# A state-space convolution beside grouped attention: the output projection of the last queries is summed ahead of the last norm

## The chip, the cores and the metric

The program runs on one core of a Trainium2 chip. Its time is device microseconds from launch to end. TensorE (PE in the profile) multiplies, VectorE (DVE) and ScalarE (ACT) work on elements, GpSimd (POOL) has a few small steps, and SyncE (SP) issues DMA transfers. Products land in PSUM, eight banks of 128 x 512 fp32.

## The reference, cut to what matters

Two independent halves are computed from two inputs of 2048 x 640 and written side by side.

```python
# A: diagonal state-space layer, complex
Lam_bar = exp(dt * Lam);  B_bar = ((Lam_bar - 1) / Lam)[:, None] * Bmat
h[t] = Lam_bar * h[t-1] + (x @ B_bar.T)[t]          # 2048 steps
a = 2 * real(h @ Cmat.T) + x * Dskip
# B: 32 query heads of 20, one key and one value head
q = (x @ wq) as 32 heads;  k = x @ wk;  v = x @ wv
p = softmax(q @ k.T * 20 ** -0.5)                   # 32 x 2048 x 2048
b = concat_heads(p @ v) @ wo
out = concat([a, b], -1)                            # 1 x 2048 x 1280, bf16
```

## The kernel before, in words

**Attention.** Queries are cut into four blocks of 512 (`qb`), heads into eight groups of four (`gg`). One block of 512 queries and four heads is a block `b` (32 of them), and has 64 score tiles of 128 keys x 512 queries, 2048 tiles in all; `tile_n` counts them. TensorE multiplies keys and queries into the score banks: slot SC0 has three banks, slot SC1 two. ACT takes a whole slot in one exponential (line 1000) and writes bf16 weights to one of seven buffers PR. About one tile in five goes to a miscellaneous bank instead, where DVE makes the exponential by integer arithmetic (line 553: one instruction from PSUM, three corrections from SBUF, into buffers DR). TensorE multiplies all weights by the values, four heads side by side, into the bank `pvbank` (MB2), with one column for the softmax's denominator.

**Norm.** When a block's 64 tiles are summed, DVE copies the bank to `pvsb` (line 1190). For 31 blocks the denominators travel through DRAM and back (`normalize`, four DMA steps) and DVE multiplies them in, `norm_op[b]`, into a buffer OT. For the last block it is done on the chip, to be quicker: `den_task` brings the denominators to rows (product with E1), DVE takes the reciprocal, POOL spreads each of the 16 numbers of a row over 32 columns (rdT to rdX, line 1244), `norm_task` turns that back with a product with ident, and DVE multiplies.

**Output projection.** `o_task(qb, k, bank)` makes one output tile: k = 0 to 3 are 128 rows x 512 columns, k = 4 is the last 128 columns of all four row blocks. Each sums over the eight groups `gg` with products of OT and WO4. A product with 128 stationary columns is issued as four of 32 columns side by side (`mm`, line 528). `finish` copies the bank to one of four staging buffers (DVE, line 1298) and issues the write on SP (line 1301).

**State-space half.** Per block of 512 time steps: `unit_task` (inputs by B, rotated, scanned on DVE) and `y_task` (states by C, `finish`).

**What sets the order.** Nothing is looped at run time: `Schedule.run` plays the program with fixed durations, and each engine picks the ready step of lowest `prio` (ties by age). What it picked becomes the static instruction list of each engine, and `Emitter` adds the semaphore waits. An engine then runs its list strictly in order. Scores have priority 0, exponentials 0.5, attention products 2.0 (`PV`, line 1056), background products 1.6 (`TASK`). `background` lists the background tasks with the tile number from which they may start; state-space tasks are spread from tile `SSM_FROM` to `SSM_TO`. `manager` gives a task one of two miscellaneous banks; while one is in use the second goes only to tasks overdue by `OVERDUE` tiles. `keep_source` (line 603) adds filler products (VZ by KT, 256 columns) where TensorE's load of the last 3 us is under `KEEP`.

In this order, before, the end is: last exponential, three attention products, the copy to pvsb, the norm's steps, then all five output tiles of the last block, their copies and writes in turn in the two miscellaneous banks.

Of the kernel before, what the change touches and what calls it, by code (L numbers as in the profile page):

```python
# [8 lines left out]
ACT = mybir.ActivationFunctionType  # L9
# [350 lines left out]
NQB, NKC, NGG = 4, 16, 8  # L360
NTILE = NQB * NGG * NKC * 4
# [5 lines left out]
class Build:  # L367
# [230 lines left out]
                  load=512.0, deps=[self.zero_op], reads=["PR0"], writes=[self.pvbank.key], hook=self.warm_last)  # L598


    KEEP = 3200.0

    def keep_source(self):

# [3 lines left out]
        if self.pv_filled[b] == 64 and sum(len(q) for q in self.pvq[b]) < 12:  # L608
            return None
        if self.s.recent(3000.0) > self.KEEP:  # L610
            return None
# [334 lines left out]
    def attention(self):  # L946
# [10 lines left out]
        while self.tile_n < NTILE:  # L957
# [14 lines left out]
            fill = self.pe([], self.mmt(512, 2), deps=deps, prio=0, mode="S", hook=lambda op, i=i: self.fill(op, i))  # L972
            k += 1

    def fill(self, op, i):
        p = self
        t, banks = self.slots[i]
        n = min(self.CHUNKS[i], NTILE - self.tile_n)
        h = self.hold[self.nhold % self.NPS]
        self.nhold += 1  # L980
        tiles = list(range(self.tile_n, self.tile_n + n))
        self.tile_n += n
        extra = []
        while len(tiles) < 4 - len(extra) and self.want_d(len(extra)):
            tiles.append(self.tile_n)
            self.tile_n += 1
            extra.append(min(tiles, key=self.d_weight))
            tiles.remove(extra[-1])
            self.d_per[extra[-1] // 64, extra[-1] % 4] += 1
        ents = []  # L990
        for x, m in enumerate(tiles):
            b, kc, j = self.score(op, m, t[:, 512 * x:512 * x + 512], banks[x])
            ents.append((b, kc, j, p.PR[:, h.index, x, :]))
        for m in extra:
            self.fill_d(op, m)
        op.reads = sorted(set(op.reads))
        op.dur = self.mmt(512, len(op.fns))
        op.load = 128.0 * len(op.fns)
        dst = p.PR[:, h.index, 0:n, :]
        ex = self.act(lambda e: e.activation(dst, t[:, 0:512 * n], ACT.Exp, scale=1.0 / UNIT),  # L1000
                      0.8333 * 512 * n + 50,
                      deps=[op], reads=[b.key for b in banks[:n]], writes=[f"PR{h.index}"], prio=0.5,
                      gate=lambda: not h.taken or (h.left == 0 and self.s.done(h.users)))

        def on_start(_):
            h.taken, h.left, h.users, h.waits = True, n, [], False
        h.waits = True
        ex.hook = on_start
        self.slot_last[i] = [ex]
        for b, kc, j, rhs in ents:  # L1010
            self.pvq[b][j].append((p.VP[:, kc, 0:32], kc, rhs, f"PR{h.index}", ex, h, "VP"))
            self.pv_filled[b] += 1
# [217 lines left out]
    def den_task(self, b, bank):  # L1230

        p = self
        slot = b % 2
        src = p.pvsb[:, slot, :]
        m1 = self.pe([self.mm(bank.cols(4 * i, 4 * i + 4), src[:, 128 * i:128 * i + 128], p.E1[:], True, True)
                      for i in range(4)], 4 * 65, deps=[self.evac_op[b], self.c_op["E1"]] + bank.last, prio=1.5,
                     reads=[f"pvsb{slot}", "E1"], writes=[bank.key])

        def rc(e):
            with p.nc.allow_low_precision("bf16 reciprocal of softmax denominator"):  # L1240
                return e.reciprocal(p.rdT[:], bank.cols(0, 16))
        r = self.dve(rc, 170, deps=[m1], reads=[bank.key], writes=[f"rdT{slot}"], prio=0.45)
        spread = bass.AP(tensor=p.rdT, offset=0, ap=[[16, 128], [1, 16], [0, 32]])
        self.spread_op[b] = self.pool(lambda e: e.tensor_copy(p.rdX[:], spread), 700, deps=[r],
                                      reads=[f"rdT{slot}"], writes=[f"rdX{slot}"], prio=1)
        yield lambda: r.start is not None
        bank.last = [r]
        self.give(bank)
# [16 lines left out]
        self.give(bank)  # L1265

    def o_task(self, qb, k, bank):
        p = self
        ops = self.o_ops.setdefault(qb, [])
        prev = None  # L1270
        ots = [(8 * qb + gg) % 10 for gg in range(NGG)]
        deps = [self.norm_op[8 * qb + gg] for gg in range(NGG)] + [self.wo_op] + bank.last
        if k < 4:
            for gg in range(NGG):
                prev = self.pe([self.mm(bank.ap, p.OT[:, ots[gg], 128 * k:128 * k + 128], p.WO4[:, gg, 0:512], gg == 0,
                                        gg == NGG - 1)], self.mmt(512), deps=deps, prev=prev, prio=self.task_prio(),
                               reads=[f"OT{ots[gg]}", "WO4"], writes=[bank.key])
            rows = self.out[0, 512 * qb + 128 * k:512 * qb + 128 * k + 128, 640:1152]
        else:
            for ts in range(4):  # L1280
                for gg in range(NGG):
                    prev = self.pe([self.mm(bank.cols(128 * ts, 128 * ts + 128),
                                            p.OT[:, ots[gg], 128 * ts:128 * ts + 128], p.WO4[:, gg, 512:640], gg == 0,
                                            gg == NGG - 1)], 65, deps=deps, prev=prev, prio=self.task_prio(),
                                   reads=[f"OT{ots[gg]}", "WO4"], writes=[bank.key])
            rows = self.out[0, 512 * qb:512 * qb + 512, 1152:1280].rearrange("(t p) n -> p t n", p=128)
        ev = self.finish(prev, rows, bank, ops)
        yield lambda: ev.start is not None
        self.give(bank)

    def finish(self, prev, rows, bank, ops):

        ops.append(prev)
        i = self.outs % 4
        self.outs += 1
        key, st = f"stg{i}", self.stg[:, i, :]
        last = self.stage_dma.get(key)
        ev = self.dve(lambda e: e.tensor_copy(st, bank.ap), 620, deps=[prev], reads=[bank.key], writes=[key], prio=self.EV,  # L1298
                      gate=(lambda: last.end is not None and last.end + 100 < self.s.t) if last else None)
        src = st if len(rows.shape) == 2 else st.rearrange("p (t n) -> p t n", t=4)  # L1300
        self.stage_dma[key] = self.dma(lambda e: e.dma_start(rows, src), 131072, f"out{i}", deps=[ev], reads=[key],
                                       prio=1)
        bank.last = [ev]
        return ev

# [237 lines left out]
        return lambda: o is None or o.start is not None  # L1543


    SSM_FROM, SSM_TO = 130, 1960

    def background(self):
        T = self.tasks
        for qb in range(NQB):  # L1550
            for gg in range(NGG):
                t = -100 + gg if qb == 0 else (qb - 1) * 512 + 40 + 50 * gg
                T.append((t, 1, lambda b=8 * qb + gg: self.tile_n >= 64 * (b - 11), lambda bank, qb=qb, gg=gg: self.qt_task(qb, gg, bank)))
                if gg % 4 == 3:
                    T.append((t + 0.5, 0, lambda qb=qb, gg=gg: self.row_ready(qb, gg),
                              lambda bank, qb=qb, gg=gg: self.row_task(qb, gg // 4, bank)))
# [3 lines left out]
                T.append((64 * (b + 1), 0, lambda b=b: self.norm_ready(b), lambda bank, b=b: self.norm_task(b, bank)))  # L1560
        for qb in range(NQB):
            for k in range(5):
                T.append((512 * (qb + 1) + 30 + 40 * k, 2, lambda qb=qb: self.o_ready(qb),
                          lambda bank, qb=qb, k=k: self.o_task(qb, (4, 0, 1, 2, 3)[k], bank)))
        jobs = []
        for tb in range(NQB + 1):
# [29 lines left out]
        return self.ot_free(b)  # L1596

    def o_ready(self, qb):
        return all((8 * qb + gg) in self.norm_op and self.norm_op[8 * qb + gg].start is not None for gg in range(NGG))

    def unit_ready(self, tb, c, ri):
        if ri == 1:
# [11 lines left out]
        return all((tb, c) in self.w_op and self.w_op[(tb, c)].start is not None for c in range(NC))  # L1614

    in_use = 0
    OVERDUE = 80

    def manager(self):
        tasks = self.tasks  # L1620

        def choose():
            if not any(b in self.misc for b in self.free_banks):
                return None
            late = self.tile_n - self.OVERDUE if self.started and self.in_use > 0 else 1e9
            best = None
            for i, (t, cls, ok, gen) in enumerate(tasks):
                if t > self.tile_n and self.tile_n < NTILE:
                    break
                if t > late and cls > 0:  # L1630
                    continue
                if (best is None or cls < tasks[best][1]) and ok():
                    best = i
            return best
        while tasks:
            yield lambda: choose() is not None
            i = choose()
            bank = self.take(self.misc)
            self.in_use += 1
            bank.task = True  # L1640
            _, _, _, gen = tasks.pop(i)
            self.s.spawn(gen(bank))
            yield lambda: True
# [50 lines left out]
```

## Time and profile before

| | us |
|---|---|
| median of 7 runs (lowest, highest) | 801.0 (800.76, 805.16) |
| the profiled execution | 801.24 |
| its span, first to last instruction | 799.5 |
| ACT busy | 769.8 |
| TensorE busy, DVE busy | 731.5, 729.8 |
| POOL busy | 14.1 |
| mean granted TensorE clock | 0.998 of full |

The span lies 1.7 us under the profiled execution's own time, and that 0.24 above the median. Busy times are sums over stages with different limits; records of one engine can overlap, since a following instruction starts while the one ahead drains. A profile line gives source line, engine, operation, written tile <- read tiles, shape, count, then busy time and mean ns of one. Line 538 holds nearly all products of the helper `mm`, line 534 those issued in fours, so they are told apart by their tiles: SC and MB are banks, WO,OT the output projection, PR,VP and DR,VS attention sums, E,pvsb and ident,rdX the last norm.

### The profile page before, as it was taken

The numbers are of one execution on the slowest core, as the hardware profiler recorded it, in microseconds if no ns is written. First come the engines' busy times: TensorE is split into PE (matmuls) and PEld (weight loads), VectorE is DVE, ScalarE is ACT, GpSimd is POOL, SyncE is SP. The second block draws the span as 40 slices with busy tenths as digits, with TensorE's granted clock in tenths as the row PEclk, the third lists the DMA queues.
The fourth block names the chain that finished last, engine by engine and source line by source line (L and its number), as shares of the span: only waits on it lengthen the run. The fifth ranks groups of instructions, "written<-read, shape, count | busy, mean of one in ns | idle before, by whom it ended". The sixth has DMA issues, their size and how long they took to land.

```text
span 799.5 us, 23698 instructions
## 1 busy us (share of the span) xinstructions
PE 731.5 (91%) x10175; PEld 237.8 (30%) x10177; DVE 729.8 (91%) x1779; ACT 769.8 (96%) x689; POOL 14.1 (2%) x36
## 2 busy tenths in 40 slices
PE   7989898989889999999899999999988999989986
PEld 3322222222224233222323223223222322223323
DVE  5999999999998988998998999999999899997692
ACT  5899999999999999999999999999999999999991
POOL 6000000000000000000000000000000000000000
PEclk9999999999999999999999999999999999999999
DMA  9830020000001000010000000020000100000101
GB/s 206 128 77 8 17 43 9 7 4 10 8 9 24 22 16 22 16 33 25 15 2 23 22 23 23 5 45 16 10 15 9 29 15 22 15 9 16 29 16 35
DMA packets 54185, 21.57 MB, mean 27 GB/s; under 512 B 43464, under 2 KB 54080, under 8 KB 54080
## 3 DMA queue, kind: packets, MB, share of 16 engines
q1 hardware_dynamic: 52072, 19.87, 11.5%
q8 instruction: 80, 1.31, 0.7%
q10 hardware_dynamic: 2008, 0.18, 0.3%
q14 instruction: 25, 0.20, 0.1%
HBM read 7.20 MB, written 5.50 MB: 16 GB/s over the span
## 4 chain that ended last, share of the span: by engine, by line
issue 96%; PE 1%; DVE 1%; DMA 1%; ACTq 0%; POOL 0%; POOLq 0%; DVEq 0%
PE MB L534 1%; DMA vrow<-in_A_Dskip_dram 1%; DVE xbT L760 0%; DVE fr L553 0%; POOL fr L553 0%; ACTq L519 0%; DVE wq L748 0%; DVE OT L548 0%; DVE stg L1298 0%; POOLq L425 0%; DVE aq L552 0%; DVE mab L781 0%; ACTq L518 0%; DVE sc L552 0%; DVE trig L552 0%
## 5 line engine op out<-in xcount | busy, mean ns | idle before, releaser
L1000 ACT ACTIVATE PR<-SC 128x1536 bf16<-128x1536 f32 (+1 forms) x667 | 754.7, 1459 | 4.7 <-PE SC L538 2.5
L538 PE MATMUL SC<-QT,KT 32*128 32x512 bf16 x1668 | 259.9, 384 | 53.0 <-ACT PR L1000 42.3
L553 DVE TENSOR_SCALAR DR<-MB 128x512 int16<-128x512 f32 x380 | 255.2, 685 | 29.3 <-PE MB L538 27.5
L538 PE MATMUL MB<-PR,VP 128*32 128x512 bf16 x1668 | 250.9, 385 | 1.7 <-DVE pvsb L1190 0.7
L538 PE MATMUL MB<-DR,VS 128*32 128x512 bf16 x1520 | 247.0, 384 | 0.7 <-DVE DR L553 0.4
L553 DVE TENSOR_SCALAR DR<-DR 128x512 int16<-128x512 int16 (+1 forms) x849 | 238.3, 333 | 4.0 <-PE MB L538 1.8
L538 PEld LDWEIGHTS SC<-QT,KT 32*128 32x128 bf16 x1668 | 66.9, 91 | 307.9 <-ACT PR L1000 243.4
L538 PE MATMUL MB<-QT,KT 32*128 32x512 bf16 x380 | 139.7, 384 | 1.9 <-DVE DR L553 1.4
L538 PEld LDWEIGHTS MB<-PR,VP 128*32 128x32 bf16 x1668 | 60.6, 94 | 65.8 <-issue 51.7
L538 PEld LDWEIGHTS MB<-DR,VS 128*32 128x32 bf16 x1520 | 59.6, 94 | 56.4 <-issue 42.6
L534 PE MATMUL MB<-xaT,BT 128*32 128x512 bf16 x800 | 61.6, 382 | 0.6 <-DVE QT L881 0.3
L548 DVE TENSOR_TENSOR prod<-MB,Z 128x1024 bf16<-128x1024 f32 x40 | 48.8, 1221 | 5.6 <-PE MB L534 5.3
L538 PE MATMUL MB<-xbT,wqf 128*32 128x512 bf16 x640 | 48.5, 382 | 0.4 <-DVE QT L881 0.3
L534 PE MATMUL MB<-WO,OT 128*32 128x512 bf16 (+1 forms) x1024 | 46.9, 311 | 0.4 <-DVE OT L548 0.4
L538 PEld LDWEIGHTS MB<-QT,KT 32*128 32x128 bf16 x380 | 33.0, 91 | 22.0 <-issue 10.7
L1470 DVE TENSOR_TENSOR_SCAN g<-sc,hst,u 128x512 bf16<-128x512 f32 x30 | 37.9, 1276 | 0.0
L1298 DVE CAST stg<-MB 128x512 bf16<-128x512 f32 x40 | 27.4, 686 | 8.1 <-PE MB L534 7.9
L538 PE MATMUL MB<-KT,VZ 128*32 128x256 bf16 x628 | 32.9, 275 | 0.0
L534 PE MATMUL MB<-CT,xbT 128*32 128x512 bf16 (+1 forms) x640 | 31.0, 300 | 0.1
L534 PE MATMUL MB<-CT,W 128*32 128x512 bf16 (+1 forms) x640 | 30.5, 301 | 0.0
L548 DVE TENSOR_TENSOR prod<-g,tab 128x1024 bf16<-128x1024 bf16 x40 | 27.1, 681 | 0.1
L1190 DVE CAST pvsb<-MB 128x512 bf16<-128x512 f32 x32 | 21.9, 686 | 4.0 <-PE MB L538 3.5
(116 smaller groups left out, 332.3 us busy)
## 6 DMA issues: line engine op xcount, KB each, us to landing
out_dram<-stg SPq DMA_DIRECT2D x40, 128.0 KB, 1.8
rdB<-recs SPq DMA_DIRECT2D x124, 32.0 KB, 1.9
CT<-in_B_x_dram SPq DMA_DIRECT2D x2, 640.0 KB, 5.6
WO<-in_B_wo_dram SPq DMA_DIRECT2D x4, 200.0 KB
wqf<-in_B_wq_dram SPq DMA_DIRECT2D x1, 680.0 KB, 5.9
sums<-pvsb SPq DMA_DIRECT2D x31, 4.0 KB
dn<-sums SPq DMA_DIRECT2D x31, 4.0 KB, 2.0
recs<-rc SPq DMA_DIRECT2D x31, 4.0 KB, 1.6
```

Of the source, the lines that this page charges most:

```text
L534: r = e.matmul(out[32 * j:32 * j + 32], lhsT=lhsT[:, 32 * j:32 * j + 32], rhs=rhs, start=start, stop=stop, tile_position=(0, 32 * j), skip ...
L538: return lambda e: e.matmul(out, lhsT=lhsT, rhs=rhs, start=start, stop=stop, **kw)
L548: return lambda e: e.tensor_tensor(out, a, b, op)
L553: return lambda e: e.tensor_scalar(out, a, s1, s2, op0=op0, op1=op1)
L1000: ex = self.act(lambda e: e.activation(dst, t[:, 0:512 * n], ACT.Exp, scale=1.0 / UNIT), 0.8333 * 512 * n + 50, deps=[op], reads=[b.key fo ...
L1190: ev = self.dve(lambda e: e.tensor_copy(p.pvsb[:, slot, :], bank.ap), 620, deps=[op], reads=[bank.key], writes=[f"pvsb{slot}"], prio=self. ...
L1298: ev = self.dve(lambda e: e.tensor_copy(st, bank.ap), 620, deps=[prev], reads=[bank.key], writes=[key], prio=self.EV, gate=(lambda: last.e ...
L1470: o = self.dve(lambda e, ri=ri, init=init: e.tensor_tensor_scan(p.g[:, u, ri, :], rdec, p.u[:, ri, :], init, ALU.mult, ALU.add), 1280, dep ...
```

## The change

- Output tiles of the last query block (`last`, qb = 3) may start once the first group is normed, from tile 2040 on, and each group's products wait for that group's norm alone. k = 4 goes group by group instead of row block by row block. The products have priority 2.5 (1.4 for the last group).
- After the last scores of a slot have been taken by ACT, the slot's banks join the miscellaneous ones, so more output tiles can be open at once. The limit by `OVERDUE` is off for the last eight tiles.
- The last block's output is staged in the free buffers PR, one for each tile. Three of the five copies (k = 4, 1, 3) are made by ACT, two by DVE.
- The spread of the reciprocals (rdT to rdX) goes from POOL to DVE.
- `KEEP` 3200 to 3500, `SSM_FROM, SSM_TO` 130, 1960 to 110, 1830, `OVERDUE` 80 to 120.

```diff
-    KEEP = 3200.0
+    KEEP = 3500.0
...
+        for i in (k % 2, (k + 1) % 2):
+            yield lambda: fill.start is not None and all(o.start is not None for o in self.slot_last[i])
+            for bank in self.slots[i][1]:
+                bank.last, bank.busy = list(self.slot_last[i]), False
+                self.misc.append(bank)
+                self.free_banks.append(bank)
...
-        self.spread_op[b] = self.pool(lambda e: e.tensor_copy(p.rdX[:], spread), 700, deps=[r],
+        self.spread_op[b] = self.dve(lambda e: e.tensor_copy(p.rdX[:], spread), 350, deps=[r],
...
+        last = qb == NQB - 1
+        def part(gg, prev):
+            fns = []
+            for ts in range(4) if k == 4 else [k]:
+                out, w = (bank.cols(128 * ts, 128 * ts + 128), p.WO4[:, gg, 512:640]) if k == 4 else (bank.ap, p.WO4[:, gg, 0:512])
+                fns.append(self.mm(out, p.OT[:, ots[gg], 128 * ts:128 * ts + 128], w, gg == 0 and ts in (0, k), gg == NGG - 1))
+            return self.pe(fns, 4 * 65 if k == 4 else self.mmt(512), deps=[self.norm_op[8 * qb + gg], self.wo_op] + bank.last,
+                           prev=prev, prio=1.4 if last and gg == NGG - 1 else 2.5 if last else self.task_prio(),
+                           reads=[f"OT{ots[gg]}", "WO4"], writes=[bank.key])
+        for gg in range(NGG):
+            if last:
+                yield lambda: 8 * qb + gg in self.norm_op
+            prev = part(gg, prev)
...
-        ev = self.finish(prev, rows, bank, ops)
+        ev = self.finish(prev, rows, bank, ops, k if last else None)
...
+        else:
+            key, st = f"PR{end}", self.PR[:, end, 0, :]
...
+        if end in (4, 1, 3):
+            ev = self.act(lambda e: e.activation(st, bank.ap, ACT.Copy), 600, deps=[prev], reads=[bank.key], writes=[key], prio=1)
...
-    SSM_FROM, SSM_TO = 130, 1960
+    SSM_FROM, SSM_TO = 110, 1830
...
-                T.append((512 * (qb + 1) + 30 + 40 * k, 2, lambda qb=qb: self.o_ready(qb),
+                T.append((512 * (qb + 1) + 30 + 40 * k if qb < NQB - 1 else NTILE - 8, 2, lambda qb=qb: self.o_ready(qb),
...
-        return all((8 * qb + gg) in self.norm_op and self.norm_op[8 * qb + gg].start is not None for gg in range(NGG))
+        ggs = range(NGG if qb < NQB - 1 else 1)
+        return all((8 * qb + gg) in self.norm_op and self.norm_op[8 * qb + gg].start is not None for gg in ggs)
...
-    OVERDUE = 80
+    OVERDUE = 120
...
-            late = self.tile_n - self.OVERDUE if self.started and self.in_use > 0 else 1e9
+            late = self.tile_n - self.OVERDUE if self.started and self.in_use > 0 and self.tile_n < NTILE - 8 else 1e9
```

More of the change, by code (lines that the diff above doesn't have):

```diff
@@ L1271, in o_task @@
         ots = [(8 * qb + gg) % 10 for gg in range(NGG)]
-        deps = [self.norm_op[8 * qb + gg] for gg in range(NGG)] + [self.wo_op] + bank.last
+        last = qb == NQB - 1
[7 more added lines that the diff above has]
+                           reads=[f"OT{ots[gg]}", "WO4"], writes=[bank.key])
@@ L1273, in o_task @@
+        for gg in range(NGG):
+            if last:
+                yield lambda: 8 * qb + gg in self.norm_op
+            prev = part(gg, prev)
         if k < 4:
[L1274 to L1277, printed above, removed]
@@ L1278, in o_task @@
             rows = self.out[0, 512 * qb + 128 * k:512 * qb + 128 * k + 128, 640:1152]
         else:
[L1280 to L1285, printed above, removed]
@@ L1286, in o_task, with finish @@
             rows = self.out[0, 512 * qb:512 * qb + 512, 1152:1280].rearrange("(t p) n -> p t n", p=128)
-        ev = self.finish(prev, rows, bank, ops)
+        ev = self.finish(prev, rows, bank, ops, k if last else None)
         yield lambda: ev.start is not None
         self.give(bank)
-    def finish(self, prev, rows, bank, ops):
+    def finish(self, prev, rows, bank, ops, end=None):
         ops.append(prev)
-        i = self.outs % 4
-        self.outs += 1
-        key, st = f"stg{i}", self.stg[:, i, :]
-        last = self.stage_dma.get(key)
-        ev = self.dve(lambda e: e.tensor_copy(st, bank.ap), 620, deps=[prev], reads=[bank.key], writes=[key], prio=self.EV,
-                      gate=(lambda: last.end is not None and last.end + 100 < self.s.t) if last else None)
+        if end is None:
+            i = self.outs % 4
+            self.outs += 1
+            key, st = f"stg{i}", self.stg[:, i, :]
+        else:
+            key, st = f"PR{end}", self.PR[:, end, 0, :]
+        last = self.stage_dma.get(key)
+        if end in (4, 1, 3):
+            ev = self.act(lambda e: e.activation(st, bank.ap, ACT.Copy), 600, deps=[prev], reads=[bank.key], writes=[key], prio=1)
+        else:
+            ev = self.dve(lambda e: e.tensor_copy(st, bank.ap), 620, deps=[prev], reads=[bank.key], writes=[key], prio=self.EV,
+                          gate=(lambda: last.end is not None and last.end + 100 < self.s.t) if last else None)
@@ L1300, in finish @@
         src = st if len(rows.shape) == 2 else st.rearrange("p (t n) -> p t n", t=4)
-        self.stage_dma[key] = self.dma(lambda e: e.dma_start(rows, src), 131072, f"out{i}", deps=[ev], reads=[key],
-                                       prio=1)
+        self.stage_dma[key] = self.dma(lambda e: e.dma_start(rows, src), 131072, f"out{key}", deps=[ev], reads=[key], prio=1)
         bank.last = [ev]
```

## The prediction

> **What bounds the kernel now.** I read the page first, then the groups kept apart by shape, then the timeline of the last 20 us engine by engine, then windows of the TensorE clock.
>
> ```profile
> PE 731.5 (91%) x10175; PEld 237.8 (30%) x10177; DVE 729.8 (91%) x1779; ACT 769.8 (96%) x689; POOL 14.1 (2%) x36
> ```
>
> ScalarE (ACT) leads, but 91% on two others says little before the stages are separated. In the groups (busy, mean ns | idle before, by whom):
>
> ```profile
> L1000 ACT ACTIVATE PR<-SC 128x1536 bf16<-128x1536 f32 x334 | 557.5, 1669 | 4.0 <-PE SC L538 2.5 <-PE MB L538 1.4
> L1000 ACT ACTIVATE PR<-SC 128x1024 bf16<-128x1024 f32 x333 | 415.4, 1247 | 0.6 <-PE MB L538 0.6
> ...
> L538 PEld LDWEIGHTS SC<-QT,KT 32*128 32x128 bf16 x1668 | 66.9, 91 | 307.9 <-ACT PR L1000 243.4 <-DVE DR L553 40.0 <-issue 10.3
> ```
>
> From 25.33 us (first exponential) to 782.55 (last) ACT runs 667 exponentials with hardly a gap, and TensorE waits for ACT before new scores: the main stage is ACT's. Overlapping records hide part of its loss. Start to start, the trace never has under 1.330 us after a three-bank exponential nor under 0.904 after a two-bank one: 333 pairs x 2.234 = 743.9 us, against 780.79 - 25.33 = 755.5. So 11.5 us of waiting lie in the main stage (the longest single one 1.24 us, near 487). After it:
>
> ```profile
> 778.54 4.01 ACT L1000 ACTIVATE PR<-SC 128x1536 bf16<-128x1536 f32 x3
> ```
> ```profile
> 782.61 0.40 PE L538 MATMUL MB<-PR,VP 128*32 128x512 bf16 x3 [0.51 <-ACT PR L1000]
> 783.80 0.26 PE L534 MATMUL MB<-E,pvsb 128*32 128x4 bf16 x16 [0.79 <-DVE pvsb L1190]
> 785.12 0.41 PE L534 MATMUL MB<-ident,rdX 128*32 128x128 bf16 x16 [1.06 <-POOL rdX L1244]
> 785.36 0.56 PE L534 MATMUL MB<-WO,OT 128*32 128x128 bf16 x28
> 786.33 10.13 PE L534 MATMUL MB<-WO,OT 128*32 128x128 bf16 x228 [0.40 <-DVE OT L548]
> ```
> ```profile
> 785.58 0.69 DVE L548 TENSOR_TENSOR OT<-pvsb,MB 128x512 bf16<-128x512 bf16 x1 [1.19 <-PE MB L534]
> 789.21 0.69 DVE L1298 CAST stg<-MB 128x512 bf16<-128x512 f32 x1 [2.94 <-PE MB L534]
> 791.33 0.69 DVE L1298 CAST stg<-MB 128x512 bf16<-128x512 f32 x1 [1.43 <-PE MB L534]
> 793.05 0.69 DVE L1298 CAST stg<-MB 128x512 bf16<-128x512 f32 x1 [1.03 <-PE MB L534]
> 794.78 0.69 DVE L1298 CAST stg<-MB 128x512 bf16<-128x512 f32 x1 [1.03 <-PE MB L534]
> 796.50 0.69 DVE L1298 CAST stg<-MB 128x512 bf16<-128x512 f32 x1 [1.03 <-PE MB L534]
> ```
>
> Call the end of the last exponential E = 782.55. The tail is 799.52 - 782.55 = 16.97 us with ACT idle: 3.78 to the first product after the last norm, 10.13 of output products, 0.05 + 0.69 for the last copy, 2.32 for the last write and the closing waits. Part of the 10.13 ran on half a clock (below).
>
> **The tail, in the changed kernel's order.** The built order is a list, and says which products stand ahead of which wait. I price it in groups of four column-tiled products. A 512-column group is 1.72/8 = 0.216 us (a round of eight groups between two copies above). A 128-column group is (785.36 - 785.12)/4 = 0.06, by start to start 0.056, and twice that on half a clock.
>
> (1) Before E. The exponential before the last ends at E - 1.34. Behind it TensorE has one attention group (0.22), 16 output groups of 128 columns (0.89) and one of 512 (0.22): with the hop of 0.05 done at about E + 0.03. The last attention products, which wait for E, are reached just in time; if they are late, that adds one to one.
>
> (2) Last attention products. Before, three stood behind E (one group); now thirteen, four groups: TensorE free at E + 0.05 + 0.86 = E + 0.91, the sum complete near E + 1.09 instead of E + 0.45. Cost 0.64. DVE's copies that they also wait for should be done by E - 1 (nine DVE instructions, 4.3 us of rows, follow a score filled at about E - 6.8).
>
> (3) Norm. Output groups now fill the three gaps of the chain, five each time, 1.08 us: behind the attention sum, behind the small product with E1, behind the product with ident. The old gaps were 0.79 + 0.22, 1.06 and 0.40 + 0.56 us, so the fillings are a little longer than the waits and TensorE sets the pace: E1 at 0.91 + 1.08 = E + 1.99, +0.11, +1.08, ident at E + 3.18, +0.23, +1.08: ready for the last norm at E + 4.49. The chain by itself, 783.00 to 786.33 = 3.33 less what the spread saves, would be ready at 1.09 + 3.12 = E + 4.21; so 4.49 holds.
>
> (4) The spread moves from POOL (0.61) to DVE. No row is a copy that repeats each element 32 times. Bounds: 0.29 (the 128x512 int16 form of line 553) and 0.69 (a 512-column cast); I take 0.42, the two-operand bf16 row of line 548, as it lies between: 0.2 saved. At 0.69 it would be about 0.2 later than the filling, otherwise hidden by it. [...] No row here shows the case, and the sum changes by at most 0.2.
>
> (5) After the last norm. The words of the change promise one group of each output tile; the order gives more. Of the third 512-wide tile only two of the seven earlier groups stand ahead of the norm's wait, of the fourth none; they are queued behind it though they do not need it. So: 4 groups of 128 (0.22), 1 + 7 + 8 = 16 groups of 512 (3.45), 0.17 for the last result: E + 8.33. Before: 796.46 = E + 13.91.
>
> (6) Copies and writes. Three copies go to ACT (0.59 by the 128x512 copy of line 763), two to DVE; each result is further from the next than a copy takes, or goes to the other engine, so only the last counts: 0.05 + 0.59, E + 8.97. SP issues five writes of 0.33 to 0.40 us in this order, none late. The staging names grow from 4 to 9, so SP's closing waits (two names per instruction, 0.06 each) grow by at most 0.15; I take 0.1. End: E + 8.97 + 2.32 + 0.1 = E + 11.4. Tail 16.97 - 11.4 = **5.6 us less**.
>
> The clock of the tail is a second term: full clock is assumed above. Windows of before show (us, TensorE busy, granted clock, DMA share, GB/s):
>
> ```profile
> 786.80:787.30 0.50, 0.50 (x31) 0.50 0.00 0
> 787.30:787.80 0.50, 0.50 (x32) 0.50 0.17 33
> ...
> 789.30:789.80 0.50, 0.50 (x9) 0.50 0.00 0
> 789.80:790.30 0.50, 0.50 (x16) 1.00 0.00 0
> ```
>
> Half speed from about 786.4 to 789.8, after 3.4 us with many gaps; it cost 3.4/2 = 1.7 us. With the gaps filled I expect none of it; if it comes all the same, 1.7 is to be added. [...]
>
> **The main stage.** The counts do not move: 334 + 333 exponentials and 380 scores on DVE in both orders, so ACT's floor of 743.9 stays. What moves is the waiting of 11.5 us:
> - Fillers rise from 628 to 892, 66 more groups of 0.12 us = 7.9 us of TensorE. They stand where it would idle (it waits 243 us for ACT). The clock was 1.00 all through, so they buy nothing; a filler in the wrong place costs one 0.12.
> - DVE: 82 more single copies (0.287) and 41 fewer double (0.420): +6.3 us; three copies fewer in the tail, -2.1; one spread, +0.4. From 729.8 to about 734 of the 757 us of the stage: covered, but the cover is thin, 98.0 of 100 us in the window from 100 to 200.
> - The state-space work (about 179 us of DVE by its rows) goes into 1720 tiles instead of 1830, at 0.37 us a tile 636 us instead of 676: 28% of DVE instead of 26.5% there, less after it. Its writes move earlier through SP, 0.35 us each, past the norm chains' small transfers.
> - TensorE's work between two score fills, counted from both orders with the prices above: 22 pairs of fills longer than ACT's 2.234 us before, 26 after, with about the same excess.
>
> None of this fixes the sign. I take zero, bounds -4 (a third of the waits goes) and +4.
>
> **Sum.** Against the profiled execution (801.24 us for a span of 799.5): 801.2 - 5.6 = 795.6; the median of the seven runs is 0.24 lower, so **795.4**.
>
> **Rivals.**
> A (0.62): as above, the main stage within 2.4 us of before: 793 to 798.
> B (0.16): the looser end of the state-space work also takes waits out of the main stage, 4 of the 11.5: 791.4. For it: the six waits of 0.5 us and more make 4.6 us, and lie where that work is dense. Against: the work is packed denser there.
> C (0.13): the gain is there and eaten: the half clock in the tail (1.7) and 2 us of new waits, 795.4 + 3.7 = 799.1, no change. For it: steps 1 to 3 leave no slack.
> D (0.09): slower. DVE becomes the bound in the stretch of the denser state-space work, at 100 to 650 us: late copies hold back attention products, these hold the exponentials' buffers, ACT waits. If the 11.5 us double, 795.4 + 11.5 = 806.9. It decides once it takes 5.6 + 2.4 = 8 us. Against: the order gives DVE no more scores than before.
>
> A measurement of this kernel can tell about 0.3%, 2.4 us. Faster by more: A and B, 0.78; within: 0.13; slower: 0.09. The range takes in the bounds of the main stage: 795.4 - 4 and 795.4 + 4 with some of C: 791.5 to 799.8.
>
> **What would show it.** In the changed profile: the tail from the last exponential about 11.4 us; the first product after the norm about E + 4.5 and 3.7 us of output products behind it; PEclk 1.00 there; rdX on DVE near 0.42; the last exponential ending within 2.4 us of 782.55. I am wrong if that end moves by more than 4 us, if the clock halves again, or if the thirteen attention products start later than E + 0.3.

## The result and the profile after

| | before | after |
|---|---|---|
| median, us (lowest, highest; runs) | 801.29 (799.65, 805.16; 45) | 798.36 (795.95, 802.12; 17) |
| ratio of the times, with its 95% interval | | 0.9958 [0.9948, 0.9968] |
| the profiled execution | 801.24 | 799.93 |
| its span | 799.52 | 798.20 |
| of it: up to the first exponential | 25.33 | 25.37 |
| main stage, first exponential to the end E of the last | 757.22 | 761.62 |
| tail, E to the last instruction | 16.97 | 11.21 |

The change makes the kernel 0.42% faster; 0.7% was forecast. The last three rows say where the rest is: the tail is 5.75 us shorter, and the main stage, which the change was not about, is 4.40 us longer.

The page's busy times, and the exponentials kept apart by shape (count | busy, mean ns | idle before, by whom):

```profile
PE 736.5 (92%) x10439; PEld 240.6 (30%) x10441; DVE 732.0 (92%) x1818; ACT 772.2 (97%) x692; POOL 13.5 (2%) x35
```
```profile
L1007 ACT ACTIVATE PR<-SC 128x1536 bf16<-128x1536 f32 x334 | 555.4, 1663 | 6.8 <-PE SC L538 4.8 <-PE MB L538 2.0
L1007 ACT ACTIVATE PR<-SC 128x1024 bf16<-128x1024 f32 x333 | 413.1, 1240 | 1.6 <-PE MB L538 1.0 <-PE SC L538 0.6
```

The same 334 + 333 exponentials, so ACT's floor of 743.9 us stands; the idle time before them grew from 4.6 to 8.4 us. By starts (over 1.330 and 0.904 us) the waits are 15.99 us against 11.54.

**The tail.** TensorE's timeline from E = 786.99 on (start, us, source <- tiles, count):

```profile
787.04 0.39 PE L538 MATMUL MB<-PR,VP 128*32 128x512 bf16 x1
...
787.72 1.45 PE L534 MATMUL MB<-WO,OT 128*32 128x512 bf16 x18
788.89 0.31 PE L534 MATMUL SC<-E,pvsb 128*32 128x4 bf16 x10
...
789.26 1.09 PE L534 MATMUL SC<-WO,OT 128*32 128x512 bf16 x16
790.14 0.44 PE L534 MATMUL SC<-ident,rdX 128*32 128x128 bf16 x16
790.37 1.28 PE L534 MATMUL SC<-WO,OT 128*32 128x512 bf16 x20
791.45 0.64 PE L534 MATMUL MB<-WO,OT 128*32 128x128 bf16 x20
791.89 3.44 PE L534 MATMUL SC<-WO,OT 128*32 128x512 bf16 x60
```

No line has an idle time in brackets, where before there were four: WO,OT fills the three gaps of the norm's chain, and 80 products (20 groups) are left behind the norm. DVE's spread and ACT's last copy:

```profile
789.65 0.43 DVE L1251 COPY rdX<-rdT 128x512 bf16<-128x512 bf16 x1
```
```profile
795.38 0.60 ACT L1314 ACTIVATE PR<-SC 128x512 bf16<-128x512 f32 x1 [2.37 <-PE SC L534]
```

**The main stage.** The long waits of ACT stand at new places: 1.03, 1.04 and 1.00 us at 63.6, 65.5 and 68.8, then 0.99 and 1.34 at 96.9 and 100.5. Windows of 3.41 us (TensorE busy, granted clock, DMA share, GB/s):

```profile
55.81:59.22 3.41, 3.41 (x50) 1.00 0.04 8
59.22:62.63 3.41, 2.21 (x31) 1.00 0.02 1
62.63:66.04 3.41, 3.41 (x27) 0.50 0.12 41
66.04:69.45 3.41, 3.41 (x30) 0.50 0.00 0
69.45:72.86 3.41, 3.33 (x45) 1.00 0.02 5
...
93.36:96.77 3.41, 2.21 (x31) 1.00 0.24 65
96.77:100.18 3.41, 3.41 (x34) 0.50 0.71 132
```

Twice TensorE is busy for only 2.21 of 3.41 us, and the clock is half for one or two windows after it: a fill of two score banks then takes 0.60 us (0.39 at full clock), and ACT waits. Before, the main stage had no window at half clock. What TensorE lacked in the two thin windows is in the timelines of SP, DVE and TensorE:

```profile
56.96 0.51 SPq L1215 DMA_DIRECT2D dn<-sums  x1
```
```profile
60.37 0.34 DVE L1220 RECIPROCAL rc<-dn 64x32 bf16<-64x32 bf16 x1 [1.36 <-DMA dn<-sums]
...
92.16 2.19 DVE L683 MEMSET WO<- 128x2560 uint32 x1 [0.48 <-issue]
```
```profile
62.18 0.38 PE L538 MATMUL MB<-QT,KT 32*128 32x512 bf16 x1 [1.01 <-DVE QT L881]
...
95.48 0.38 PE L538 MATMUL MB<-QT,KT 32*128 32x512 bf16 x1 [1.01 <-DVE DR L553]
```

First: a block's denominators took 3.4 us from issue to landing (2.4 before). DVE reaches the reciprocal 2.05 us after the issue, about as before (2.16), so it waits 1.36 us (0.27 before), is late with the copies behind it (QT and DR), and TensorE idles 1.01 us. So here the late landing made the wait, and not the reciprocal's place in the list. Second: DVE zeroes WO4 in 2.19 us, where `Schedule.run` counted 1.5. DVE's exponential that frees a miscellaneous bank stands behind that (94.74 us), and TensorE idles 1.01 us before the next score for that bank.

The 17 times go with the granted clock: the four runs at clock 1.000 took 795.95 to 796.38 us, five at 0.996 took 798.3 to 798.67, two of the three at 0.994 took 799.93 and 799.99. One window at half rate is 0.002 of the mean clock (half of 3.41 us in 798), so each goes with 1.0 to 1.3 us, its cause included. Most times around the median are those of runs with two (the median run itself, 798.36 us at 0.998, shows one).

### The profile page after: what moved, and what is told of

Read it like the earlier page. It is cut to its first block, busy times and chain, and to the rows that moved or that the text cites. A ratio compares the mean times of both kernels' runs of the same rounds, so it can differ in the third digit from the quotient of the medians.

```text
span 798.2 us, 24288 instructions
## 1 busy us (share of the span) xinstructions
PE 736.5 (92%) x10439; PEld 240.6 (30%) x10441; DVE 732.0 (92%) x1818; ACT 772.2 (97%) x692; POOL 13.5 (2%) x35
## 3 DMA queue, kind: packets, MB, share of 16 engines
q8 instruction: 82, 1.34, 0.7%
## 4 chain that ended last, share of the span: by engine, by line
ACT 82%; PE 10%; DVE 5%; DMA 1%; issue 1%; SPq 0%; ACTq 0%; DVEq 0%
ACT PR L1007 82%; PE MB L538 4%; PE SC L538 3%; DVE DR L553 3%; PE MB L534 2%; PE SC L534 1%; DMA vrow<-in_A_Dskip_dram 1%; DVE prod L548 0%; DMA dn<-sums 0%; SPq L927 0%; DVE WO L683 0%; DVE xbT L760 0%; DMA sums<-pvsb 0%; ACTq L519 0%; DVE fr L553 0%
## 5 line engine op out<-in xcount | busy, mean ns | idle before, releaser
L553 DVE TENSOR_SCALAR DR<-MB 128x512 int16<-128x512 f32 x380 | 255.3, 685 | 24.8 <-PE MB L538 22.9
L538 PE MATMUL MB<-PR,VP 128*32 128x512 bf16 x1668 | 254.4, 386 | 1.5 <-DVE pvsb L1197 1.3
L538 PE MATMUL MB<-DR,VS 128*32 128x512 bf16 x1520 | 254.2, 387 | 0.6 <-DVE pvsb L1197 0.6
L553 DVE TENSOR_SCALAR DR<-DR 128x512 int16<-128x512 int16 (+1 forms) x890 | 243.2, 325 | 7.7 <-PE MB L538 4.5
L534 PE MATMUL MB<-xaT,BT 128*32 128x512 bf16 x800 | 62.9, 387 | 0.0
L538 PE MATMUL MB<-KT,VZ 128*32 128x256 bf16 x892 | 43.5, 276 | 0.0
L534 PE MATMUL MB<-WO,OT 128*32 128x128 bf16 (+1 forms) x928 | 42.4, 292 | 0.0
L538 PEld LDWEIGHTS MB<-QT,KT 32*128 32x128 bf16 x380 | 33.1, 91 | 22.2 <-issue 12.1
L1316 DVE CAST stg<-MB 128x512 bf16<-128x512 f32 x35 | 23.9, 684 | 3.9 <-PE MB L534 3.5
L538 PEld LDWEIGHTS MB<-KT,VZ 128*32 128x32 bf16 x892 | 22.1, 96 | 12.7 <-issue 6.4
```

Source lines behind the costliest of these rows:

```text
L534: r = e.matmul(out[32 * j:32 * j + 32], lhsT=lhsT[:, 32 * j:32 * j + 32], rhs=rhs, start=start, stop=stop, tile_position=(0, 32 * j), skip ...
L538: return lambda e: e.matmul(out, lhsT=lhsT, rhs=rhs, start=start, stop=stop, **kw)
L553: return lambda e: e.tensor_scalar(out, a, s1, s2, op0=op0, op1=op1)
```

## The experiments

Theory 1: the tail's edits bring all of the forecast, and the three constants (`KEEP`, `SSM_FROM`/`SSM_TO`, `OVERDUE`) give part of it back in the main stage, by places like these two. Rivals: the tail's new order itself disturbs the main stage; or DVE becomes the bound where state-space work is packed denser (rival D).

**e1: the tail's edits alone.** The three constants as before, and the earlier query blocks' output tiles in their old order (the change's new loop also reorders their k = 4).

```diff
-    KEEP = 3500.0
+    KEEP = 3200.0
-    SSM_FROM, SSM_TO = 110, 1830
+    SSM_FROM, SSM_TO = 130, 1960
-    OVERDUE = 120
+    OVERDUE = 80
+        if not last:   # the old loops, row block by row block, all norms at once
+            ...
-        for gg in range(NGG):
+        for gg in range(NGG) if last else []:
```

> Only the tail edits (output tiles of the last queries ahead of the last norm, score banks given back, staging in PR, copies on two engines, spread on DVE); KEEP, SSM_FROM, SSM_TO and OVERDUE as before, and earlier query blocks' output tiles in their old order. The instruction lists of all engines are those of the kernel before up to TensorE's instruction 9836 of 10162. Theory 1 (the tail gives its gain, the three constants lose some of it in the main stage): last exponential ends within 1 us of 782.6; behind it one attention group instead of four in the changed kernel, so the tail is 16.97 - 10.5 = 6.4 us shorter than before; ratio 0.992, and better than the changed kernel's 0.9958. Theory 2 (the tail edits themselves hold the main stage up): last exponential near 787 and a ratio near 0.996.

Measured: 794.6 us, ratio 0.9927 [0.9915, 0.9938]. Waits 11.61 us at the places of before, main stage 757.30 (before 757.22), tail 10.56. The tail's edits cost the main stage nothing. The tail is also 0.65 us shorter than in the changed kernel: one group of attention products stands behind E here, not four.

**e2: the constants alone**, in the kernel before.

```diff
-    KEEP = 3200.0
+    KEEP = 3500.0
-    SSM_FROM, SSM_TO = 130, 1960
+    SSM_FROM, SSM_TO = 110, 1830
-    OVERDUE = 80
+    OVERDUE = 120
```

> The kernel before with only the constants of the change: KEEP 3500, SSM 110 to 1830, OVERDUE 120. Theory 1: main stage 2 to 4.5 us longer, half-rate windows of TensorE in the first 110 us in most runs, tail as before: ratio 1.003 to 1.005. Theory 2: 1.000.

Measured: 803.06 us, ratio 1.0032 [1.0020, 1.0045]. In its profile the main stage is 1.25 us longer than before (waits 1.02 and 1.14 us at 93.9 and 97.3, half clock from 94.3 to 97.7) and the tail 0.74 (a second window at half clock). 2 to 4.5 us of main stage were expected, so that part was missed. The parts add up in time: -0.73% and +0.32% make -0.41%, and the whole change measured -0.42%. They do not add up place by place, since the 0.74 us lie in a tail that the changed kernel does not have, so that the sum is this close is in part chance.

**e3: the second place mended.** The changed kernel, same order; DVE zeroes five of the eight parts of WO4, GpSimd the other three.

```diff
-        ... self.dve(lambda e: e.memset(p.WO4[:], 0.0), 1500, writes=["WO4"], ...
+        ... self.dve(lambda e: e.memset(p.WO4[:, 0:5, :], 0.0), 1500, writes=["WO4"], ...
+        self.pool(lambda e: e.memset(p.WO4[:, 5:8, :], 0.0), 2000, writes=["WO4b"], ...
```

> The changed kernel, all instruction lists of TensorE, DVE and ACT unchanged, but the zeroing of WO4 on DVE (2.19 us near 92 us, which the planner counts as 1.5) is cut to five eighths of its columns, about 1.4 us; GpSimd zeroes the rest early. Theory 1 with this instruction as one of its causes: TensorE's idle time of 1.0 us near 94.5 shrinks to 0.3 or less, the clock stays 1.00 from 96 to 101, and ACT's two waits there (0.99 and 1.34) go: 1 to 2.3 us faster than the changed kernel, ratio 0.993 to 0.995. Rival: the clock halves there for another reason, or the time is lost elsewhere later: ratio 0.996 unchanged.

Measured: 796.51 us, ratio 0.9947 [0.9936, 0.9959]. The profile has no window at half clock, waits 11.16 us, main stage 756.79, tail 11.21. TensorE has no idle time of 1 us near 94, so the second place is mended. The waits near 63 to 71 are gone too, though nothing was done for them: with the same lists the transfer to dn took 1.9 us here and not 3.4, and the reciprocal waited for nothing. So the first place depends on when that transfer lands. All five runs show a clock of 0.998 or 1.000, as 7 of the 17 of the changed kernel do; but the two ratios' intervals overlap, so the gain in time is likely and not shown beyond the noise. The edit also costs something: the first exponential starts at 26.43 us, 1.06 late. While GpSimd zeroes its part of WO4 (from 18.34 us, for 1.69), one of DVE's instructions ahead of the first scores (line 553, into fr) takes 2.48 us, where the same one took 0.85 in the changed kernel; in e5, with the same edit, it takes 2.49.

**e4: the first place mended in the plan.** `Schedule.run` counts the transfer to dn 1 us longer, so that the reciprocal is planned later.

```diff
-                     reads=[f"sums{b}"], writes=[dn], prio=1)
+                     reads=[f"sums{b}"], writes=[dn], prio=1, land=1000.0)
```

> The changed kernel, but the planner counts the second transfer of the denominators (sums to dn) as landing 1 us later, so that DVE's reciprocal stands later in its list and the list is no longer held up when the transfer is late (1.36 us near 59 in the profiled run). The order of everything behind changes. Theory 1 with this wait as one of its causes: no wait of DVE for dn, no half-rate window near 62 to 69, ACT's three waits there (1.03, 1.04, 1.00) go: ratio 0.992 to 0.994. Rival (each new order brings its own waits): those waits go and others come, ratio 0.996 plus or minus 0.003.

Measured: 801.23 us, ratio 1.0005 [0.9993, 1.0016]: worse than either reading. The order is another one throughout. DVE takes 372 scores and not 380, so ACT does 8 more (about 8 x 0.45 = 3.6 us), and there are waits of 0.73, 0.63 and 0.64 us at 62.9 to 67.4 around a window at half clock all the same. Nor did the edit do what it was for: the transfer took 1.8 us, but was issued later (58.69 us), DVE reached the reciprocal 0.51 us after the issue and waited 1.33 us for it. So e4 says nothing on what the first place is worth.

**e5: e1 with e3's edit.**

```diff
-        ... self.dve(lambda e: e.memset(p.WO4[:], 0.0), 1500, writes=["WO4"], ...
+        ... self.dve(lambda e: e.memset(p.WO4[:, 0:5, :], 0.0), 1500, writes=["WO4"], ...
+        self.pool(lambda e: e.memset(p.WO4[:, 5:8, :], 0.0), 2000, writes=["WO4b"], ...
```

> The tail edits alone (as e1_tail_pure), and the zeroing of WO4 on DVE cut to five eighths, the rest early on GpSimd; no list of TensorE or ACT changes. If DVE's late zeroing also causes the waits of the exponentials near 100.0 (0.75) and 104.4 (0.77) that e1 and the kernel before share, both go: 1 to 1.5 us less than e1, ratio 0.991. If it causes only the first: 0.992. If neither: 0.9927 as e1.

Measured: 796.7 us, ratio 0.9939 [0.9923, 0.9956]. Of the two waits of 0.75 us at 100 and 104 one is gone, but the waits in sum (11.68 us against 11.61) and the main stage (757.37 against 757.30) are those of e1, and the first exponential comes 1.46 us later (26.38 against 24.92), by e3's side effect. So this edit brings e1 nothing and costs the late start.

**e6: e1 without fillers.**

```diff
-    KEEP = 3200.0
+    KEEP = -1.0
```

> The tail edits alone, without any filler products (612 in e1, none here); the planner's order changes from TensorE's instruction 468 on. The prediction's view (the fillers buy nothing where the clock is full): clock 0.998 or more, time within 0.3% of e1, ratio 0.990 to 0.996. Rival (the fillers hold the clock up): half-rate windows in the main stage, at 1.2 to 1.4 us each; with four or more of them a clock of 0.99 and a ratio of 0.998 or more.

Measured: 815.38 us, ratio 1.0163 [1.0136, 1.0189]. 612 filler products less, and mean clock, waits (34.5 us) and main stage (779.30 us) are all worse:

```profile
core 0: 815.2 us, clock 0.952
```

A clock of 0.952 over 815.2 us is worth 23 windows of 3.41 us at half clock. The waits grew by 22.9 us, one of 3.99 of them at 57.4, behind constants that DVE waited for:

```profile
55.09 0.99 DVE L552 TENSOR_SCALAR CT<-CT 128x3200 bf16<-128x3200 bf16 x1 [4.54 <-DMA CT<-in_A_C_im_dram]
```

The order is not e1's in other respects either, so not all 22.9 us are the clock's. But the prediction's sentence that fillers buy nothing, since the clock was 1.00 all through, has it the wrong way round: with them it was 1.00 (e1's profile), without them it is 0.952.

**e7: e1 with the output tiles open from 24 tiles before the end**, not 8.

```diff
-    ... else NTILE - 8, 2, lambda qb=qb: self.o_ready(qb),
+    ... else NTILE - 24, 2, lambda qb=qb: self.o_ready(qb),
-            ... and self.tile_n < NTILE - 8 else 1e9
+            ... and self.tile_n < NTILE - 24 else 1e9
```

> The tail edits alone, but the last output tiles may start 24 score tiles before the end instead of 8. Four more score tiles go to ACT instead of DVE (1672 against 1668), 4 x 0.43 = 1.7 us of ACT; behind the last norm stand 1 + 2 + 2 groups of 512 columns instead of 16, 2.4 us less of TensorE, and three more attention groups behind the last exponential, 0.5 us. If the tail is bound by TensorE as worked out: tail about 8.5 us instead of 10.6, last exponential 1 to 2 us later, net 0.2 to 1 us less than e1, ratio 0.9915 to 0.9925. Rival: the waits between the norm's steps set the tail and not TensorE's products: tail 10 or more, slower than e1 by 1 us.

Measured: 797.09 us, ratio 0.9946 [0.9929, 0.9962], by the ratios 1.5 us over e1, with intervals that overlap. Behind the norm only 36 products are left, and the tail is 10.16 us, 0.4 shorter and not the 2 expected:

```profile
790.49 0.64 PE L534 MATMUL MB<-WO,OT 128*32 128x128 bf16 x20
790.92 1.06 PE L534 MATMUL SC<-WO,OT 128*32 128x512 bf16 x16
```

All five results are now ready within 1.5 us, and queue for copies (the last ends at 792.64) and for SP, whose fifth write is issued at 793.78. And the main stage is 3.6 us longer: the open tiles hold the miscellaneous banks that DVE's scores use (two exponentials more on ACT), and a wait of 1.10 us at 340.8 follows a window at half clock.

**e8: one engine for the copies.** e1 with all five copies on DVE and the spread on POOL.

```diff
-        self.spread_op[b] = self.dve(lambda e: e.tensor_copy(p.rdX[:], spread), 350, deps=[r],
+        self.spread_op[b] = self.pool(lambda e: e.tensor_copy(p.rdX[:], spread), 700, deps=[r],
-        if end in (4, 1, 3):
+        if False:
```

> The tail edits alone, but all five last copies on DVE and the spread of the reciprocals on GpSimd as before. If the order of the products makes the gain, the tail grows by 0.1 (copy 0.69 against 0.60) to 0.3 us: 10.7 to 10.9, ratio 0.993. Rival (the second engine and the quicker spread make a good part of it): tail 11.5 or more, ratio 0.994 or more.

Measured: 795.36 us, ratio 0.9920 [0.9904, 0.9935], tail 10.65 us against 10.56. The second engine and DVE's spread together are worth 0.1 us. What shortens the tail is the order of the products, with the banks and staging that it needs; these were not tried apart.

**e9, e10, e11: e1 with one of the three constants each.**

```diff
-    KEEP = 3200.0                  # e9
+    KEEP = 3500.0
-    SSM_FROM, SSM_TO = 130, 1960   # e10
+    SSM_FROM, SSM_TO = 110, 1830
-    OVERDUE = 80                   # e11
+    OVERDUE = 120
```

> The tail edits alone with KEEP 3500 in place of 3200 (820 fillers against 612). The run without fillers showed that they hold the clock up, so more of them should not lower it: clock 0.998 or more. If the change's loss in the main stage (2.6 us for the three constants together) is this constant's: ratio 0.995 to 0.996. If it helps, as more cover for the clock: 0.990 to 0.992. If each new order merely brings waits of its own: 0.9927 plus or minus 0.002.

> The tail edits alone with the state-space work spread from tile 110 to 1830 in place of 130 to 1960. If the denser state-space work loads DVE too much (rival D of the prediction): waits of the exponentials spread over 100 to 650 us and a ratio of 0.995 or more. If not: 0.9927 plus or minus 0.002, with waits at other places.

> The tail edits alone with OVERDUE 120 in place of 80. Five more scores go to DVE (385 against 380), 2.1 us less for ACT. If the second miscellaneous bank is what this frees: ratio 0.990. If it delays query products so that TensorE idles in the first 110 us, as in the changed kernel: half-rate windows there and 0.994 to 0.996.

| us | ratio | main stage | tail | waits |
|---|---|---|---|---|
| e1 | 0.9927 [0.9915, 0.9938] | 757.30 | 10.56 | 11.6 |
| e9, KEEP | 0.9928 [0.9908, 0.9947] | 757.89 | 10.78 | 13.1 |
| e10, SSM | 0.9922 [0.9902, 0.9942] | 757.03 | 10.77 | 11.8 |
| e11, OVERDUE | 0.9992 [0.9978, 1.0007] | 756.14 | 17.33 | 12.7 |

Neither KEEP nor the denser state-space stretch costs anything that shows. OVERDUE costs 0.65 points, which was neither of the two expected cases, and by its profile it costs them in the tail: its main stage is even the shortest (DVE takes 385 scores). There state-space tasks, put off longer, reach the end. TensorE's timeline, with E at 781.0:

```profile
780.64 2.33 PE L534 MATMUL MB<-CT,xbT 128*32 128x512 bf16 x40
...
783.02 2.33 PE L534 MATMUL SC<-CT,xbT 128*32 128x512 bf16 x40
785.18 0.40 PE L534 MATMUL SC<-diagD,xaT 128*32 128x128 bf16 x16
785.41 0.60 PE L538 MATMUL MB<-PR,VP 128*32 128x512 bf16 x6
```

The last attention products stand behind two output tiles of the state-space half and start at E + 4.4, not E + 0.05. With `SSM_TO` = 1830, as in the change, these tasks are over long before (the last CT,xbT product starts at 705 us), so the later bound and the earlier stretch belong together.

**e12: the changed kernel with OVERDUE back at 80**, the other two constants as changed.

```diff
-    OVERDUE = 120
+    OVERDUE = 80
```

> The changed kernel with one constant put back: the overdue bound of the planner (OVERDUE) 80 again instead of 120; the fillers' gap of 3500 and the state-space stretch of 110 to 1830 stay as the change has them. Theory 1 (the overdue bound is what costs in the main stage): ratio 0.992 to 0.993, the long waits of ScalarE near 63 to 71 us and at 97 and 100 us are gone, TensorE has no idle time of 1.0 us near 61 and 94 us, the last exponential ends near 782 us and the tail takes 10.5 to 11.2 us. Rival (every new order of the tasks has late arrivals of its own, whichever constant makes it): ratio 0.995 to 0.996, waits of ScalarE of 13 us or more in sum, at places of their own, with at least one stretch of half clock before 110 us.

Measured: 795.11 us (794.39 to 795.40), ratio 0.9920 [0.9907, 0.9934], main stage 757.81, waits 12.1, tail 10.55. Time, E (782.84) and tail are theory 1's. At the first place the reciprocal waits 0.19 us. Three state-space steps of DVE stand ahead of it, but DVE still reaches it 1.66 us after the issue, sooner than in the changed kernel (2.05): it is the transfer that was quick (1.8 us).

```profile
59.55 0.34 DVE L1220 RECIPROCAL rc<-dn 64x32 bf16<-64x32 bf16 x1 [0.19 <-DMA dn<-sums]
```

One thing is the rival's: a single window at half clock, from 94.8 to 98.3 us, with waits of 0.5 to 0.65 around it. So with the other two constants in place OVERDUE = 120 costs 0.9958 - 0.9920 = 0.38 points, about 3 us. It is not shown that the bound is bad by itself (e11's main stage speaks against that), nor that the half clock makes all of it: in runs at clock 1.000 the changed kernel took 795.95 to 796.38 us and e12 794.39 and 794.51. So 1.4 to 2 of the 3 us are there without any half clock; 0.66 of them are the tail (11.21 against 10.55), and the rest was not traced to a place. What is shown is that the order that OVERDUE = 120 leads to here costs the time and that another (e12) gives it back; and that at the second place a DVE step longer than planned leads to a thin window, since it goes when the step is cut (e3). e1, e8, e9, e10 and e12 all beat the changed kernel, and cannot be told apart by their intervals.

## Why the prediction was right, and where not

The sign, the range (791.5 to 799.8) and the tail were right; the size was too large by 3.0 us (795.4 against 798.36). The case that came is rival A's tail with an eaten part as in C, but eaten in the main stage. That the range held is in part luck: 4 of the 17 runs, the profiled one among them, lie above 799.8, and how many windows at half clock a run has depends in part on when a transfer lands (3.4 us in the profile, 1.9 in e3, with the same lists).

Steps of the tail, relative to E, forecast and measured:

| step | forecast | measured |
|---|---|---|
| (1, 2) last attention products start | 0.05 | 0.05 |
| (3) product with E1 | 1.99 | 1.90 |
| (3) product with ident | 3.18 | 3.15 |
| (4) spread on DVE, duration | 0.42 | 0.43 |
| (5) first product behind the norm | 4.49 | 4.46 |
| (5) last result ready | 8.33 | 8.34 |
| (6) last copy done | 8.97 | 8.99 |
| end | 11.4 | 11.21 |

Every step holds within 0.1 us and the sum within 0.2, since the built order said which products stand ahead of which wait, and each kind had a row in the trace. Reading the order also caught what the description of the change left out: 20 groups behind the norm, not five. In (6), e8 shows that the two engines hardly matter, in line with the step's "only the last counts".

The spread's 0.42 us was an estimate from the two-operand bf16 row, between bounds of 0.29 and 0.69 from two other rows; the 0.43 measured lies close to it.

The clock term of the tail was right too: 1.00 in all windows from 770 to 793 us. Its price of 1.7 us, which the sum did not need, was somewhat high: in the runs beside the experiments the kernel before took 800.9 us in the median at a clock of 0.998, which is one window at half rate, and 799.6 at 1.000.

**The step that failed is the main stage, taken as zero.** It measured +4.40 us in the profiled run, past the bound of 4 and past the "4 us" that the prediction named as its own refutation (E went from 782.55 to 786.99). By the runs' median it was about +3: some 2 us of half clock and about 1 besides. Three sentences of that step were off:

- "The clock was 1.00 all through, so they buy nothing": e6 shows what fillers buy. It also hid the risk: a half clock was weighed only for the tail, while the thinnest window of the main stage before, 2.32 of 3.41 us of TensorE (591.8 to 595.2 us, the next one still at 1.00), lies just above the 2.21 after which the changed kernel's clock was half.
- DVE's cover was called thin, but only its sum was weighed. What mattered was where a single DVE instruction waits or runs longer than `Schedule.run` counts (1.36 us for a transfer, 2.19 for 1.5), and who is queued behind it.
- Fillers, state-space stretch and DVE's load got a paragraph each; `OVERDUE` got none, and it is what costs: in the tail without the earlier state-space stretch (e11), and 0.38 points with it (e12).

Rival D, DVE as the bound in the denser stretch, is refuted by e10 (0.9922). Rival B's gain, 4 us of waits less, is in no run: the shortest main stage, e11's, is 1.1 us under that of before.

## What to carry to other kernels

A static order holds two kinds of change: local ones, which can be priced step by step to 0.1 us from the built list, and global constants, which shuffle everything, so that sums of work do not give their price (here a good part of it came from two single places); test them apart, for here the constants gave back two fifths of what the edit had won. Where an engine's full clock depends on its being kept busy (here 1.000 in e1's profile, with 612 fillers, and 0.952 in e6's, with none), "the clock was 1.00" is a result of the order and not a property of the stage: look for the stretch in which the busy share is lowest, and ask what the change does to it. And compare the durations that a planner counts with those in the trace wherever a critical engine is queued behind them.

## What the runs showed of the hardware

- **The half clock came in whole windows on a grid.** In the changed kernel's trace the stretches at half rate are 6.83 and 3.41 us long (62.63 to 69.45, 96.77 to 100.18), and start 34.13 us apart, ten times 3.413; the one before is 3.41 us (786.39 to 789.80). With that grid laid over the main stages of both, half rate followed the two windows in which TensorE's records cover 2.21 of 3.41 us (changed kernel, 59.22 and 93.36), and no other full-rate window; all others cover 2.31 or more. It also followed 1.15 in the tail before (782.98), 0.93 in e6 (51.5) and 2.25 in e12 (91.4). The busy share is not all of it: ahead of the main stage a window of 1.85 (before, from 4.74 us) and one of 1.93 (changed kernel, from 4.60) were followed by full clock. In the changed kernel a window two thirds busy was enough: 1.0 us of waiting for DVE, with small gaps beside it, did it twice.
- **A window at half rate can hide in busy times.** In the changed kernel's three such windows TensorE's records cover 3.41 of 3.41 us. The granted clock shows them, and the count of products does too: 27 in the first, where the full-rate window ahead of the gap had 50.
- **A small transfer's time varies.** The same 4 KB to dn, at nearly the same place, took 2.4 us from issue to landing before, 3.4 after, 1.9 in e1 and 1.8 in e12; over the 31 blocks of the changed kernel's profile it took 1.8 to 3.4, in the median 1.9. With the same lists the reciprocal behind it waited 1.36 us in the changed kernel's profile and nothing in e3's, so an order without slack there can run full in one execution and not in the next.
- **A DVE step ran longer beside a GpSimd zeroing.** In e3 and e5 GpSimd zeroed 128x1920 bf16 from 18.34 and 18.30 us on, for 1.69, and the DVE step that took 0.85 us in the changed kernel (from 18.15) took 2.48 and 2.49. Why is not shown.
